# One pair of matmul products swapped in a seven-product loop, activation sums put in their order of use, and one value stage moved by a slot

## The chip, the core and the metric

The kernel runs on one core of a Trainium2 chip. The metric is the device time of that core in microseconds; the median of three executions before the change is 364.5 us (364.15 to 364.51). The profiled execution spans 361.7 us from its first to its last instruction, at a granted TensorE clock of 1.000.

## What is computed

Two layers follow each other. The first is a block-sorted attention on 4 batches of 8 heads, with sequences of 768 in 8 blocks of 96 and a head width of 64. The second is a mixture of 4 experts on the 3072 tokens that come out.

```python
# attention: P is 8x8 per head, from five rounds of row and column normalisation of exp(sort_net)
k_sorted = einsum('bhij,bhjcd->bhicd', P, k_blocks)      # blocks of keys mixed
v_sorted = einsum('bhij,bhjcd->bhicd', P, v_blocks)      # blocks of values mixed
attn = softmax(scale * q_block @ k_sorted_block.T)       # 96x96 inside each block
x = attn @ v_sorted_block                                # -> 3072 x 512

# experts: D = 512, F = 1024, E = 4
p = domain_probs / domain_probs.sum(-1)
out = sum(p[:, e] * (relu(x @ w1[e]) @ w2[e]) for e in range(4))
```

## The kernel before

The kernel's order is written out by hand: a manual schedule, in which each engine runs its instructions in the order in which the Python code emits them, and waits are put in where a tile is read, written or reused. Four batches, b = 0 to 3, have three chunks of 256 tokens each, c = 0 to 2; a chunk is also called group g = 3b + c. Attention of the next batches is computed in between the expert products of the present one. A chunk calls `slot()` after each of its pieces, and the tables `PLANS` (lines 614 to 641) say which attention stage runs in which slot: the entry `(0, 2, st_a, 2, 0)` in `PLANS[1]` runs stage `st_a` of batch 2, head pair 0, in slot 2 of chunk 0 of batch 1. The stages are `st_v` (line 357: two matmuls mix the values, ScalarE copies them to SBUF in line 367, and six small DMAs spread them into the tile `vs`), `st_k` (line 388, the keys), `st_s` (line 409: scores and exponential, two PSUM tiles), `st_a` (line 438: attention times values, one PSUM tile for each of two heads, evacuated by the `normalize` of line 427, which is a reciprocal and a multiplication on VectorE, lines 430 and 431) and `st_x` (line 457, a DMA transpose into the input of the experts). All of them take their PSUM tiles in turn from one pool with two buffers, `psA`.

The expert layers avoid part of their matmuls. Where a product of 2 x 2 blocks would take eight block products, the kernel takes seven (Strassen's method in Winograd's form) and pays with additions of blocks of weights and activations. Three pieces of code matter here.

**Chunks of batch 0 with c > 0** (`chunk`, lines 866 to 899). The second layer runs seven products by the function `times` (line 758), which accumulate over experts in four halves of PSUM banks, `bankA` to `bankQ`. The sums of activations are made by `h_sums` (line 744) on VectorE: number 1 is line 750, 2 is 752, 3 is 754, 4 is 756. The product "t2" adds into `bankA`, line 884 evacuates `bankA` into `oa2`, and the product "t3" then adds further into the same bank, so it has to wait for that evacuation. The sums number 3 and 4 stand ahead of line 884 in VectorE's queue. The product "t3" reads the sums number 3, the product "b22" behind it reads the sums number 4.

**The first layer of the last six groups** (`last_first` from line 1160, with `seven` from line 1080). Groups 6 to 11 are handled in three pairs, with one call of `last_first` for each pair and two of `last_second`. A pair has eight parts, two for each expert. Each part has seven products of four matmuls (line 1104), 128 x 128 weights by 256 columns, and three PSUM banks: X, Z (two of each, taken in turn by even and odd parts) and Q (four). The functions of a part are:

- `p1`: product into Z, then ScalarE copies Z into X (line 1124)
- `p5`: product into Q
- `p6`: product added into X, ScalarE copies X to `u2` (line 1131)
- `p2`: product added into Z, VectorE evacuates Z to the activations (`finish`, line 1110: relu and weight)
- `p7`: product added into X, ScalarE copies X to `u3` (line 1139), VectorE makes `t22` = Q + `u3` (line 1140)
- `p4`: product added into X, VectorE evacuates X (line 1110)
- `p3`: product added into Q, VectorE makes `t12` = Q + `u2` (line 1148)
- 22 and 12: `finish2` of `t22` and `t12`: relu on ScalarE (line 1116), weight on GpSimd (line 1117)

The loop of lines 1182 to 1194 interleaves a part (`now`) with the one before it (`prev`). In this document "now6" is `p6` of the present part and "prev4" is `p4` of the previous one. In the order of the code, a repeat has the products now1, prev7, now5, now2, now6, prev4, prev3, and ScalarE's order is line 1124 (now1), 1139 (prev7), 1116 (`t12`, two parts back), 1131 (now6), 1116 (`t22` of the previous part). The last part's `p7` follows the loop, and its `p4` and `p3` run inside `last_second`.

**The second layer of these groups** (`last_second`, line 1199). The products are emitted by its own `product` (line 1212, matmuls of line 1217). The fourth sums (line 1252), which overwrite the lower half of the activations, precede the third sums (line 1265). They are read by the product "b22", which comes in two portions: for the first experts ahead of the product "t3" (line 1268; `early` is 1 in the last group, else 2), for the other experts behind it (line 1282). The third sums are read by "t3".

Of the kernel before, what the change touches and what calls it, by code (L numbers as in the profile page):

```python
# [12 lines left out]
ALU = mybir.AluOpType  # L13
# [4 lines left out]
def kernel(  # L18
# [18 lines left out]
    E = moe_w1.shape[0]  # L37
# [571 lines left out]
    def st_bk(b, qd):  # L609
# [16 lines left out]
            (2, 9, st_k, 2, 0), (2, 9, st_lv, 3, 0), (2, 9, st_n, 3, 0), (2, 11, st_s, 2, 0), (2, 12, st_q, 2, 2),  # L626
        ],
        1: [
            (0, 0, st_k, 2, 1), (0, 0, st_bk, 2, 1), (0, 1, st_lk, 3, 0), (0, 1, st_n, 3, 1), (0, 2, st_a, 2, 0), (0, 2, st_q, 2, 3),
            (0, 3, st_v, 2, 2), (0, 3, st_n, 3, 2), (0, 4, st_s, 2, 1), (0, 4, st_x, 2, 0), (0, 5, st_k, 2, 2),  # L630
            (0, 5, st_n, 3, 3), (0, 6, st_v, 2, 3), (0, 6, st_lv, 3, 1), (0, 7, st_s, 2, 2), (0, 8, st_k, 2, 3),
            (0, 8, st_bv, 3, 0), (0, 9, st_bk, 3, 0), (0, 9, st_lk, 3, 1), (0, 9, st_q, 3, 0), (0, 10, st_a, 2, 1),
            (0, 11, st_s, 2, 3), (0, 12, st_a, 2, 2), (0, 12, st_x, 2, 1), (0, 12, st_q, 3, 1), (0, 13, st_v, 3, 0),
# [110 lines left out]
    def h_sums(e, which, own=False, hb=None):  # L744
        h = Hb[:, homes.get(e, e)] if hb is None else hb(e)
        blk = lambda kh, tok: h[:, ds(kh * KH, KH), ds(tok * P, P)]
        sm = [Sb[:, n, e].rearrange("p (f x) -> p f x", f=KH) for n in range(4)]
        tt = nc.vector.tensor_tensor
        if which == 1:
            tt(sm[0], blk(0, 1), blk(1, 1), ALU.add)  # L750
        elif which == 2:
            tt(sm[1], sm[0], blk(0, 0), ALU.subtract)
        elif which == 3:
            tt(blk(0, 1) if own else sm[2], blk(0, 0), blk(0, 1), ALU.subtract)
        else:
            tt(blk(1, 0) if own else sm[3], blk(1, 0), sm[1], ALU.subtract)

    def times(ps, lhs, rhs, es, first=True, done=True, between=None, at=None):

        for e in es:  # L760
            if e == at:
                between()
            for f in range(KH):
                nc.tensor.matmul(  # L764
                    ps, lhs(e, f), Ts[e][rhs][:, f, :],
                    start=(first and e == es[0] and f == 0), stop=(done and e == es[-1] and f == KH - 1),
                    skip_group_check=True,
                )
# [28 lines left out]
    def chunk(b, c, slot, done=()):  # L797
# [68 lines left out]
        if c:  # L866
            both = ob.rearrange("p (h d) -> p h d", h=2)
            times(bankA, blk(0, 0), "b11", es)
            slot()
            times(bankB, blk(1, 0), "b21", es)  # L870
            slot()
            tt(oa1, bankA, oa1, ALU.add)
            tt(oa1, bankB, oa1, ALU.add)
            h_sums(E - 1, 2)
            times(bankC, blk(1, 1), "n4", es[:1], True, False)
            times(bankQ, sm(0), "t1", es)
            tt(ob2, bankQ, ob2, ALU.add)
            slot()
            for e in es:
                h_sums(e, 3)  # L880
            for e in es:
                h_sums(e, 4)
            times(bankA, sm(1), "t2", es, False)
            tt(oa2, bankA, oa2, ALU.add)
            slot()
            next(sums0)
            times(bankC, blk(1, 1), "n4", es[1:], False)
            tt(ob1, bankC, ob1, ALU.add)
            slot()
            times(bankA, sm(2), "t3", es, False)  # L890
            tt(both, bankA.rearrange("p (o d) -> p o d", o=1).broadcast_to([P, 2, DH]), both, ALU.add)
            slot()
            store(1, ob)
            next(sums0)
            times(bankQ, sm(3), "b22", es, False)
            tt(oa2, bankQ, oa2, ALU.add)
            slot()
            store(0, oa)
            return
# [180 lines left out]
    def seven(g, n):  # L1080

        lead = g == G0
        if lead:
            e, f0, cols = n, 0, P
            pb = pbs[divmod(g, R // 2)]
            home = lambda i, j: Hb[:, e, ds(i * KH, KH), ds(j * P, P)]
            weight = lambda j: pb[:, ds(e, 1), ds(j * P, P)]
            n -= 1
            Q = last["Q"][(0, 0, 1, 3)[e]][:]
        else:  # L1090
            e, f0, cols = n // 2, n % 2 * 2, 2 * P
            home = lambda i, j: (last["H"][e] if j else Hb[:, e])[:, ds(i * KH + f0, 2), :]
            weight = lambda j: pbs[g](j, e)
            Q = last["Q"][n % 4][:]
        m = 512 // cols
        a, t = As[e], Bs[g]
        X, Z = [last[nm][n % len(last[nm])][:] for nm in ("X", "Z")]
        u2, u3, t22, t12 = [last[nm][n % len(last[nm])] for nm in ("u2", "u3", "t22", "t12")]
        tt = nc.vector.tensor_tensor

        def product(dst, lhs, rhs, first=False):
            for f in range(m):
                for k in range(2):
                    nc.tensor.matmul(  # L1104
                        dst[:, ds(f * cols, cols)], a[lhs][:, k, ds((f0 + f) * P, P)], t[rhs][:, k, :],
                        start=(first and f == 0 and k == 0), stop=(f == m - 1 and k == 1), skip_group_check=True,
                    )

        def finish(i, j, src):
            nc.vector.scalar_tensor_tensor(  # L1110
                out=home(i, j), in0=src.rearrange("p (f x) -> p f x", f=m), scalar=0.0,
                op0=ALU.max, in1=weight(j).broadcast_to([P, m, cols]), op1=ALU.mult,
            )

        def finish2(i, j, src):
            nc.scalar.activation(src, src, AF.Relu, bias=0.0, scale=1.0)  # L1116
            nc.gpsimd.tensor_tensor(  # L1117
                home(i, j), src.rearrange("p (f x) -> p f x", f=m),
                weight(j).broadcast_to([P, m, cols]), ALU.mult,
            )  # L1120

        def p1():
            product(Z, "a11", "b11", True)
            nc.scalar.copy(X, Z)  # L1124

        def p5():
            product(Q, "s1", "t1", True)

        def p6():
            product(X, "n2", "n2")  # L1130
            nc.scalar.copy(u2, X)  # L1131

        def p2():
            product(Z, "a12", "b21")
            finish(0, 0, Z)

        def p7():
            product(X, "s3", "t3")
            nc.scalar.copy(u3, X)  # L1139
            tt(t22, Q, u3, ALU.add)  # L1140

        def p4():
            product(X, "a22", "t4")
            finish(1, 0, X)

        def p3():
            product(Q, "s4", "b22")
            tt(t12, Q, u2, ALU.add)  # L1148

        return {  # L1150
            1: p1, 2: p2, 3: p3, 4: p4, 5: p5, 6: p6, 7: p7,
            22: lambda: finish2(1, 1, t22), 12: lambda: finish2(0, 1, t12),
        }

# [5 lines left out]
    def last_first(g, slot=None):  # L1160
        b, c = divmod(g, R // 2)
        lead = int(g == G0)
        if lead:
            chunk_first(b, c, [0], 0, slot)
            last_banks(0)
            last_tmp(g)
            prs = {1: seven(g, 1)}
            prs[1][1]()
            prs[1][5]()
            seven(g, 2)[5]()  # L1170
            prs[1][6]()
            prs[1][2]()
            input_sums(0, 0, True)
            input_sums(0, 1, True)
            last_banks(1)
        else:
            last["e0"][2]()
            prs = {0: last["e0"]}
        N7 = E if lead else 2 * E
        for e in range(1 + lead, N7):  # L1180
            prs[e] = seven(g, e)
        for e in range(1 + lead, N7):
            now, prev = prs[e], prs[e - 1]
            now[1]()
            prev[7]()
            if e > 1 + lead:
                prs[e - 2][12]()
            if not lead or e > 2:
                now[5]()
            now[2]()  # L1190
            now[6]()
            prev[22]()
            prev[4]()
            prev[3]()
        now[7]()
        prev[12]()
        return now

    def last_second(g, now=None, upper=False):
# [12 lines left out]
        def product(ps, lhs, rhs, first=True, es=range(E), between=None, at=E - 1, part=ds(0, DH)):  # L1212
            for e in es:
                if e == at and between:
                    between()
                for f in range(KH):
                    nc.tensor.matmul(  # L1217
                        ps, lhs(e, f), Ts[e][rhs][:, f, part],
                        start=(first and e == 0 and f == 0), stop=(e == E - 1 and f == KH - 1), skip_group_check=True,
                    )  # L1220
# [27 lines left out]
            sums(e, 2)  # L1248
        product(bankC, blk(1, 1), "n4")
        nc.scalar.copy(ob1, bankC)  # L1250
        for e in range(E):
            sums(e, 4, True)
        if lead:
            for e in range(E):
# [8 lines left out]
        if not lead:  # L1263
            for e in range(E):
                sums(e, 3, True)
        early = 1 if final else 2
        for bank, part, _ in ends:
            product(bank[:, part], blk(1, 0), "b22", False, range(early), part=part)
        if closing and not final:
# [201 lines left out]
```

The softmax here doesn't subtract the row's maximum and nothing guards it: scores larger than these inputs give would overflow.

## Time and profile before

| | |
|---|---|
| time, median of three | 364.5 us |
| span of the profiled execution | 361.7 us |
| `last_first` of the three pairs (first loop product to the first of `last_second`, by the timeline) | 211.1 to 233.4, and the same 49.4 and 98.8 us later |
| MATMUL of L1104 into X, Z, Q with 256 columns, each | 0.27 us drawn |
| ACT L1124, L1131, L1139, each | 0.57, 0.59, 0.59 us |
| ACT L1116, each | 0.63 us |
| DVE L1110, L1140, L1148, each | 0.68, 0.69, 0.68 us |
| ACT L367, each | 0.80 us |

PE is the matmul side of TensorE, PEld its loading of weights, DVE is VectorE, ACT ScalarE and POOL GpSimd. A line of the timeline gives the start of a run of equal instructions, its length to the drawn end of the last, engine, source line, operation, what it writes and reads, shapes, the number, and in brackets the idle time ahead of it with what ended that. The ends of matmuls are modelled and overlap; their starts are measured.

### The profile page before, as it was taken

The page shows a single profiled execution, that of the slowest core. Times are in us where ns is not written, and L with a number is a line of the kernel's source. Part 1 is how long each engine was busy: PE and PEld are TensorE (multiplying, and loading weights), DVE is VectorE, ACT ScalarE, POOL GpSimd, SP SyncE. Part 2 cuts the span into 40 slices and gives each one's busy share as a digit, 9 for nine tenths or more (in the row PEclk, how much of TensorE's full clock was granted, in tenths as well). Part 3 has the DMA queues.
Part 4 walks back from the last instruction along what each step waited for, and adds up shares of the span by engine and source line. Part 5 has one row for each costly group of instructions (what it writes and reads, how often), then busy time and mean ns, then how long its engine had stood idle before and what let it go on. Part 6 is the DMA issues. An engine that isn't in the chain of part 4 may idle for free.

```text
span 361.7 us, 9496 instructions
## 1 busy us (share of the span) xinstructions
PE 352.7 (98%) x3949; PEld 305.5 (84%) x3949; DVE 271.8 (75%) x549; ACT 172.6 (48%) x306; POOL 133.6 (37%) x148
## 2 busy tenths in 40 slices
PE   8799999999999999999999999999999999999995
PEld 8686857888888888988889888888888888888895
DVE  5653897769788777778878977895588876677962
ACT  2664430452324255368937158820388611688210
POOL 8872110466022330000626228840068700288300
PEclk9999999999999999999999999999999999999999
DMA  8999999999999999934994310004200015100011
GB/s 106 201 206 231 214 209 198 202 180 184 180 194 136 197 128 168 167 86 69 167 207 70 117 61 0 2 2 126 107 3 2 3 59 117 61 0 2 2 72 46
DMA packets 72007, 40.52 MB, mean 112 GB/s; under 512 B 40598, under 2 KB 66716, under 8 KB 71964
## 3 DMA queue, kind: packets, MB, share of 16 engines
q0 software_dynamic: 36560, 19.93, 41.0%
q1 hardware_dynamic: 35260, 19.92, 28.1%
q8 instruction: 31, 0.51, 0.6%
q14 instruction: 12, 0.10, 0.1%
q10 hardware_dynamic: 144, 0.07, 0.1%
HBM read 42.13 MB, written 6.34 MB: 134 GB/s over the span
## 4 chain that ended last, share of the span: by engine, by line
PE 87%; DMA 6%; DVE 3%; POOL 1%; SPq 1%; ACT 1%; issue 1%; ACTq 0%; DVEq 0%; POOLq 0%
PE ps_Q L1217 17%; PE ps_h L780 16%; PE ps_X L1104 10%; PE ps_p L764 8%; PE ps_Z L1104 7%; PE ps_Q L1104 7%; PE ps_Z L1217 6%; DMA w<-in_moe_w_dram 4%; PE ps_h L669 3%; PE ps_o L704 3%; PE ps_p L815 3%; DMA vs<-arena 2%; PE ps_a L449 1%; PE ps_s L414 1%; PE ps_v L361 1%; SPq L375 1%
## 5 line engine op out<-in xcount | busy, mean ns | idle before, releaser
L780 PE MATMUL ps_h<-xT,w 128*128 128x256 f16 x576 | 67.7, 273 | 0.0
L780 PEld LDWEIGHTS <-w 128*128 128x128 f16 x576 | 55.2, 98 | 7.3
L786 DVE SCALAR_TENSOR_TENSOR Hb<-ps_h,pb 128x1024 f16<-128x1024 f32 x34 | 41.5, 1223 | 17.1 <-PE ps_h L780 16.8
L1104 PEld LDWEIGHTS <-w 128*128 128x128 f16 x480 | 43.5, 98 | 6.4 <-issue 0.3
L1117 POOL TENSOR_TENSOR arena<-tmp,pb 128x512 f16<-128x512 f32 x12 | 15.3, 1276 | 65.8 <-PE ps_Z L1104 49.9
L1217 PEld LDWEIGHTS <-Hb 128*128 128x128 f16 x320 | 31.2, 98 | 3.6
L1116 ACT ACTIVATE tmp<-tmp 128x512 f32<-128x512 f32 x46 | 29.3, 637 | 3.2 <-DVE tmp L1148 2.6
L1217 PEld LDWEIGHTS <-Sb 128*128 128x128 f16 x304 | 28.2, 98 | 3.0
L421 ACT ACTIVATE ET<-ps_s 96x768 f16<-96x768 f32 x24 | 18.1, 802 | 25.4 <-PE ps_s L414 25.2
L1104 PEld LDWEIGHTS <-arena 128*128 128x128 f16 x312 | 27.7, 98 | 2.9
L404 ACT CAST kT<-ps_k 64x384 f16<-64x384 f32 x48 | 22.7, 473 | 14.1 <-PE ps_k L395 13.1
L121 POOL DMA_DIRECT2D arena<-in_q_dram x24 | 19.9, 840 | 19.0 <-DMA q_ring<-arena 18.4
L1104 PE MATMUL ps_X<-ET,arena 128*128 128x256 f16 x168 | 25.2, 272 | 0.0
L1124 ACT COPY ps_X<-ps_Z 128x512 f32<-128x512 f32 x27 | 15.4, 570 | 19.9 <-PE ps_Z L1104 15.6
L764 PEld LDWEIGHTS <-Hb 128*128 128x128 f16 x232 | 21.9, 98 | 3.0
L1217 PE MATMUL ps_Q<-w,Hb 128*128 128x256 f16 x192 | 24.4, 273 | 0.0
L1104 PE MATMUL ps_Z<-xT,w 128*128 128x256 f16 (+1 forms) x176 | 22.5, 258 | 0.2 <-ACT ps_X L1124 0.2
L1140 DVE TENSOR_TENSOR tmp<-ps_Q,tmp 128x512 f32<-128x512 f32 x20 | 13.8, 692 | 11.3 <-ACT tmp L1139 7.6
L1110 DVE SCALAR_TENSOR_TENSOR Hb<-ps_X,pb 128x512 f16<-128x512 f32 x27 | 18.4, 682 | 1.6 <-PE ps_X L1104 1.6
L1131 ACT COPY tmp<-ps_X 128x512 f32<-128x512 f32 x26 | 15.2, 586 | 9.0 <-PE ps_X L1104 8.7
L750 DVE TENSOR_TENSOR Sb<-Hb 128x512 f16<-128x512 f16 x33 | 19.5, 609 | 0.0
L1110 DVE SCALAR_TENSOR_TENSOR Hb<-ps_Z,pb 128x512 f16<-128x512 f32 x27 | 18.4, 682 | 1.3 <-PE ps_Z L1104 1.3
(261 smaller groups left out, 743.7 us busy)
## 6 DMA issues: line engine op xcount, KB each, us to landing
w<-in_moe_w_dram POOLq DMA_DIRECT2D x7, 1024.0 KB, 28.4
pb<-p_dram SPq DMA_DIRECT2D x9, 512.0 KB, 6.6
arena<-in_k_dram POOLq DMA_DIRECT2D x8, 384.0 KB, 10.0
arena<-in_v_dram POOLq DMA_DIRECT2D x8, 384.0 KB, 8.5
vs<-arena SPq DMA_DIRECT2D x36, 66.0 KB, 5.7
arena<-in_q_dram POOLq DMA_DIRECT2D x24, 96.0 KB, 8.1
out_dram<-ob SPq DMA_DIRECT2D x9, 256.0 KB, 2.1
out_dram<-oa SPq DMA_DIRECT2D x8, 256.0 KB, 2.3
```

What stands on the lines that cost most here:

```text
L121: nc.gpsimd.dma_start(t[:, h // 2, :, h % 2, :], q[b, h].rearrange("(t p) d -> p t d", p=P))
L404: nc.scalar.copy(kT[ds(D * hh, D), r], pk[ds(D * r, D), hh].rearrange("p a (i c) -> p a i c", c=CP),)
L421: nc.scalar.activation(ETs[2 * (pr % 2) + hh][:, 0:S].rearrange("c (a x) -> c a x", a=2), pss[hh][0:BLK, :, 0:HS], AF.Exp, bias=0.0, scale ...
L750: tt(sm[0], blk(0, 1), blk(1, 1), ALU.add)
L764: nc.tensor.matmul(ps, lhs(e, f), Ts[e][rhs][:, f, :], start=(first and e == es[0] and f == 0), stop=(done and e == es[-1] and f == KH - 1 ...
L780: nc.tensor.matmul(ps[:, f, :], w1sb[e][:, kc, ds((4 * g + f) * P, P)], xT[:, kc, ds(2 * c * P, 2 * P)], start=(kc == 0), stop=(kc == NKC ...
L786: nc.vector.scalar_tensor_tensor(out=Hb[:, homes.get(e, e), ds(4 * g, 4), :], in0=ps[:], scalar=0.0, op0=ALU.max, in1=weights(e).broadcast ...
L1104: nc.tensor.matmul(dst[:, ds(f * cols, cols)], a[lhs][:, k, ds((f0 + f) * P, P)], t[rhs][:, k, :], start=(first and f == 0 and k == 0), st ...
L1110: nc.vector.scalar_tensor_tensor(out=home(i, j), in0=src.rearrange("p (f x) -> p f x", f=m), scalar=0.0, op0=ALU.max, in1=weight(j).broadc ...
L1116: nc.scalar.activation(src, src, AF.Relu, bias=0.0, scale=1.0)
L1124: nc.scalar.copy(X, Z)
L1217: nc.tensor.matmul(ps, lhs(e, f), Ts[e][rhs][:, f, part], start=(first and e == 0 and f == 0), stop=(e == E - 1 and f == KH - 1), skip_gro ...
```

## The change

There are four edits. None adds or removes an instruction that computes; each changes places in the queues.

1. In `PLANS[1]`, `st_a` of batch 2, head pair 0, moves from slot 2 of chunk 0 to slot 3, behind the `st_v` of head pair 2 that was there. It gives the six DMAs of its values one slot more time.
2. In the chunks of batch 0 with c > 0, the product "t2" and its evacuation are emitted ahead of the fourth sums.
3. In the loop of `last_first`, for the pairs (not for group 5, the `lead` case), prev4 follows now2 directly and now6 comes behind it. The new function `p24` emits now2's product, then all of prev4 with its evacuation of X, and only then the evacuation of Z.
4. In `last_second`, again not for group 5, only the fourth sums of the first `early` experts precede the third sums; those of the other experts follow them.

```diff
-            (0, 0, st_k, 2, 1), (0, 0, st_bk, 2, 1), (0, 1, st_lk, 3, 0), (0, 1, st_n, 3, 1), (0, 2, st_a, 2, 0), (0, 2, st_q, 2, 3),
-            (0, 3, st_v, 2, 2), (0, 3, st_n, 3, 2), (0, 4, st_s, 2, 1), (0, 4, st_x, 2, 0), (0, 5, st_k, 2, 2),
+            (0, 0, st_k, 2, 1), (0, 0, st_bk, 2, 1), (0, 1, st_lk, 3, 0), (0, 1, st_n, 3, 1), (0, 2, st_q, 2, 3),
+            (0, 3, st_v, 2, 2), (0, 3, st_a, 2, 0), (0, 3, st_n, 3, 2), (0, 4, st_s, 2, 1), (0, 4, st_x, 2, 0), (0, 5, st_k, 2, 2),
...
             for e in es:
                 h_sums(e, 3)
+            times(bankA, sm(1), "t2", es, False)
+            tt(oa2, bankA, oa2, ALU.add)
             for e in es:
                 h_sums(e, 4)
-            times(bankA, sm(1), "t2", es, False)
-            tt(oa2, bankA, oa2, ALU.add)
             slot()
...
+        def p24(other):
+            product(Z, "a12", "b21")
+            other()
+            finish(0, 0, Z)
...
-            now[2]()
-            now[6]()
-            prev[22]()
-            prev[4]()
+            if lead:
+                now[2]()
+                now[6]()
+                prev[22]()
+                prev[4]()
+            else:
+                now[24](prev[4])
+                now[6]()
+                prev[22]()
             prev[3]()
...
-        for e in range(E):
+        early = 1 if final else 2
+        for e in range(E if lead else early):
             sums(e, 4, True)
...
         if not lead:
             for e in range(E):
                 sums(e, 3, True)
-        early = 1 if final else 2
+            for e in range(early, E):
+                sums(e, 4, True)
```

With that, ScalarE's order in a repeat stays as it was (lines 1124, 1139, 1116, 1131, 1116), and VectorE evacuates X ahead of Z.

More of the change, by code (lines that the diff above doesn't have):

```diff
@@ L1150, in seven @@
         return {
-            1: p1, 2: p2, 3: p3, 4: p4, 5: p5, 6: p6, 7: p7,
+            1: p1, 2: p2, 24: p24, 3: p3, 4: p4, 5: p5, 6: p6, 7: p7,
             22: lambda: finish2(1, 1, t22), 12: lambda: finish2(0, 1, t12),
```

## The prediction

> **What bounds the kernel now.** I read the page first, its busy line and then its chain.
>
> ```profile
> PE 352.7 (98%) x3949; PEld 305.5 (84%) x3949; DVE 271.8 (75%) x549; ACT 172.6 (48%) x306; POOL 133.6 (37%) x148
> ...
> PE 87%; DMA 6%; DVE 3%; POOL 1%; SPq 1%; ACT 1%; issue 1%; ACTq 0%; DVEq 0%; POOLq 0%
> ```
>
> TensorE sets the end: 98% busy, 87% of the chain, the same matmuls before and after. Only time in which it stands still between two matmuls counts. The idle column hides most of that, because a matmul is drawn 0.27 us long while full ones start 0.109 us apart. So I went to the timeline and compared starts: a product of four 256-column matmuls should take 0.44 us to the next.
>
> First, a repeat of the pair stage's loop (PE products there: L1104):
>
> ```profile
> 225.68 0.60 PE L1104 MATMUL ps_X<-ET,w 128*128 128x256 f16 x4
> 225.95 0.59 ACT L1131 COPY tmp<-ps_X 128x512 f32<-128x512 f32 x1 [0.16 <-PE ps_X L1104]
> 225.97 0.68 DVE L1110 SCALAR_TENSOR_TENSOR Hb<-ps_Z,pb 128x512 f16<-128x512 f32 x1
> ...
> 226.44 0.63 ACT L1116 ACTIVATE tmp<-tmp 128x512 f32<-128x512 f32 x1
> 226.55 0.60 PE L1104 MATMUL ps_Z<-xT,w 128*128 128x256 f16 x4
> 226.57 0.68 DVE L1110 SCALAR_TENSOR_TENSOR Hb<-ps_X,pb 128x512 f16<-128x512 f32 x1
> ...
> 227.36 0.57 ACT L1124 COPY ps_X<-ps_Z 128x512 f32<-128x512 f32 x1 [0.29 <-DVE Hb L1110]
> 227.42 0.60 PE L1104 MATMUL ps_Q<-kT,arena 128*128 128x256 f16 x4
> ...
> 227.84 0.59 ACT L1139 COPY room<-ps_X 128x512 f32<-128x512 f32 x1
> 227.98 0.60 PE L1104 MATMUL ps_Z<-xT,w 128*128 128x256 f16 x4
> ```
>
> The product at 227.98 (second of its part) should start at 227.86. It adds into Z, which L1124 copies until 227.93, and L1124 waited for DVE's eviction of X, begun at 226.57 behind that of Z. This loop of DVE and ACT takes 3.17 us (224.19 to 227.36) against 7 x 0.437 = 3.06 of products. By starts, a stage loses 0.04, 0.05, 0.12, 0.12, 0.12 in the loop and 0.04 at its last third-kind product: 0.49, in three stages 1.47 us.
>
> Second, the stage with the value change (b=1, first chunk):
>
> ```profile
> 121.23 2.35 PE L780 MATMUL ps_h<-xT,w 128*128 128x256 f16 x20
> ...
> 123.98 0.64 PE L449 MATMUL ps_a<-vs,ET 96*128 96x65 f16 x16 [0.40 <-DMA vs<-arena]
> ...
> 126.20 0.49 PE L361 MATMUL ps_v<-arena 128*128 128x384 f16 x2
> ...
> 126.77 0.80 ACT L367 CAST arena<-ps_v 128x768 f16<-128x768 f32 x1 [4.63 <-PE ps_v L361]
> ```
>
> Twenty matmuls from 121.23 end their turn at 123.41; L449 starts 0.56 later, for a DMA.
>
> Third, a chunk of b=0:
>
> ```profile
> 89.44 1.04 PE L764 MATMUL ps_p<-T,Hb 128*128 128x256 f16 x8
> ...
> 90.32 0.41 DVE L884 TENSOR_TENSOR room<-ps_p,room 128x256 f32<-128x256 f32 x1
> ...
> 90.79 1.47 PE L764 MATMUL ps_p<-T,Sb 128*128 128x256 f16 x12 [0.32 <-DVE room L884]
> ```
>
> Eight matmuls from 89.44 are through at 90.31; the next starts 0.48 later, for L884. In the next chunk the same place loses 0.18 (114.67 for 114.49).
>
> **The Trainium skill.** "PSUM — Partial Sum Buffer", Engine vs sequencer instructions: ScalarE and VectorE queues are strict FIFO, and matmuls start in program order. The trace agrees: every repeat runs L1124, L1139, L1116, L1131, L1116. The same page, PSUM bank collisions: guard PSUM by bank, so a product into X must await the whole copy out of X; here 0.05 us pass from L1124's end to the matmul (227.93 to 227.98). "ScalarE: Activation LUTs", What ACT_TABLE_LOAD costs: back-to-back ACTIVATEs overlap by about 93 ns; L1124 to L1139 shows 0.57 - 0.48 = 0.09. "Perfetto Trace Analysis", Per-engine timelines: a matmul's end is estimated, so I use starts.
>
> **The loop, part by part.** Products per repeat before: now1, prev7, now5, now2, now6, prev4, prev3. After: now1, prev7, now5, now2, prev4, now6, prev3. No instruction is added. DVE evicts X (prev4) ahead of Z (now2), which cuts the old DVE loop by 0.60: no longer the bound. But prev4 adds into the X bank that L1139 copies, and L1139 stands behind L1124. Before, three products lay between prev7 and prev4; now two. And now6 comes a product later, while its copy L1131, then a relu L1116, stand ahead of the next L1124 in ACT's queue; behind that L1124 wait now2 and everything after it on PE. This closes a new loop:
>
> - now6 to L1131: 0.71 (225.24 to 225.95)
> - L1131 to L1116: 0.48 (216.56 to 217.04; 0.49 above)
> - L1116 to L1124: back to back not in the trace. At most 0.63 + 0.08 (what L1131, with three waits, starts later behind its product than L1139 with one, 0.71 against 0.63); at least some 0.42 (0.63 less twice the overlap). I take 0.63 - 0.09 = 0.54
> - L1124 to L1139: 0.48
> - L1139: 0.59, and 0.05 to prev4
> - prev4 to now6: 0.44
>
> Sum 3.29 a repeat, 0.23 over PE's own 3.06. DVE keeps up: in a repeat it has 4 x 0.6 = 2.4.
>
> Whole stage, absolute, by the timeline from 211 us: at e=1 now2 starts at 212.37; L1139 (212.18 + 0.59 + 0.05) lets prev4 start at 212.82, now6 at 213.26. Six repeats later, the last now6 is at 213.26 + 6 x 3.29 = 233.00. The last prev7 then needs L1131's end, 0.71 + 0.59 + 0.05 = 1.35 after now6, with only prev3 between, where prev4 and prev3 were: 234.35. Before it was at 232.94. So +1.41 a stage, the old 0.49 already in it; three stages (from 211, 260 and 310) +4.23. With 0.42: +0.69 a stage; with 0.71: +2.43.
>
> **The value stage.** The group before now ends at E = 125.16 and the value product takes 0.33. The DMA is long there, so 0.56 is saved. But the pool psA has two buffers. The attention's first head takes one; its second needs the one that the value product filled, free when L367 ends: E + 0.57 + 0.80, and 0.05. Without that it starts at E + 0.57: 0.85 lost. Then 0.24 of attention, 1.75 of products: E + 3.41, where the scores' two heads need both buffers again, and TensorE with all that follows waits for them. DVE has L786 from E + 0.20 (1.13 to the next), two sums (0.44, 0.34), then two normalisations of 0.84 that ran earlier before: done at E + 3.88. The scores' second matmul, due at E + 3.5, loses 0.4. Net 0.85 + 0.40 - 0.56 = +0.69 (0.3 to 1.0).
>
> **The order of sums.** In the b=0 chunks the eviction (now ahead of three L756 sums) comes when the "t2" product ends, 89.26 in the trace, so it is over by 89.8, ahead of 90.31: -0.48, and -0.18 in the other chunk. The eviction now waits on DVE for the product's end; behind it stand the three L756 sums, L735 and L888. The sums are due only after twelve more matmuls (1.3 us against their 1.1), L888's bank only in the next group. -0.66 (-0.3 to -0.7).
>
> In the second half of the pair stages the fourth sums of late experts go behind the third sums. PE shows no wait for a sum there; its one gap, 0.23 at 354.68, is for ACT's L1262. All are still done within the 8 and 16 matmuls ahead of their use: 0.
>
> Sum: 4.23 + 0.69 - 0.66 = 4.26; 364.5 + 4.3 = 368.8.
>
> **Rivals.**
> 1. Faster: ACT overlaps so much that its loop falls under 3.06; PE never waits there. For it: the visible bound, X's eviction, is cut by 0.60. Against: ACT's sum would have to lose 0.23. -1.47 + 0.03: 363.1. Chance 0.11.
> 2. A milder loop, with the relu only 0.42 ahead of L1124: 3 x 0.69 + 0.03 = 2.1: 366.6. For it: none of the trace's ACT pairs is like this one. Chance 0.10.
> 3. A harder loop, each three-wait copy dispatched only after the relu's end: 3 x 2.43 + 0.03 = 7.3: 371.8. For it: L1131's extra 0.08. Chance 0.09.
>
> **How the numbers follow.** The main case has 0.70: 368.8, whose spread from the value stage and the sums is about 0.5 and from the loop's terms (0.03 in each of 18 repeats) 0.5. The range takes in rival 2 and ends between the main case and rival 3: 366.2 to 370.9, leaving out rival 1 and 3. Faster by over 0.2% (under 363.8): rival 1 and a little of a lucky sum, 0.12. Within: 0.04. Slower: 0.84.
>
> **What would show it.** Right: in the loop, L1124 follows an L1116 directly and no longer waits for DVE, prev4 starts 0.05 behind L1139's end, repeats last 3.3; the waits name ACT ahead of PE; L449 splits in two with a gap of 0.8 for L367; L764 follows L764 at once in the chunks of b=0. Wrong: repeats of 3.06 (ACT takes less than its rows say), or another order of ACT's instructions.

## The result and the profile after

The kernel after the change takes 368.4 us (median of six executions, 368.04 to 368.48), the kernel before 364.2 us (median of six, 362.69 to 364.51). The ratio is 1.0119 with a 95% interval of 1.0102 to 1.0137: slower by 4.2 us; 368.8 was predicted. The profiled execution spans 366.5 us against 361.7. Medians are of all executions of a kernel, while executions more than 1.5% above its fastest are left out of the ratios and of the spreads given below.

Line numbers move a little with the diff. In the kernel after, `p7`'s copy of X (1139 before) is L1144, the sums for `t22` and `t12` (1140, 1148) are L1145 and L1153, and the matmuls of `last_second` (1217) are L1227. L1104, L1110, L1116, L1124 and L1131 keep their numbers.

The page of the kernel after, its busy line and its chain:

```profile
PE 357.7 (98%) x3949; PEld 306.8 (84%) x3949; DVE 272.0 (74%) x549; ACT 170.8 (47%) x306; POOL 133.0 (36%) x148
...
PE 91%; DMA 3%; DVE 2%; ACT 1%; POOL 1%; issue 1%; ACTq 0%; DVEq 0%; POOLq 0%
```

These two lines name no new bound. The same 3949 matmuls are drawn 5.0 us longer, because most of a late start is hidden under the drawn end of the matmul ahead. The chain puts no more on ScalarE (ACT) than before. As before, the starts have to be read.

One repeat of the pair stage's loop after the change, from the timeline (start, length to the drawn end, engine, line, what is written and read):

```profile
226.63 0.60 PE L1104 MATMUL ps_X<-ET,arena 128*128 128x256 f16 x4
...
226.85 0.68 DVE L1110 SCALAR_TENSOR_TENSOR Hb<-ps_X,pb 128x512 f16<-128x512 f32 x1
...
227.34 0.58 ACT L1131 COPY tmp<-ps_X 128x512 f32<-128x512 f32 x1 [0.67 <-PE ps_X L1104]
...
227.83 0.63 ACT L1116 ACTIVATE tmp<-tmp 128x512 f32<-128x512 f32 x1
...
228.36 0.59 ACT L1124 COPY ps_X<-ps_Z 128x512 f32<-128x512 f32 x1
...
228.87 0.59 ACT L1144 COPY room<-ps_X 128x512 f32<-128x512 f32 x1
229.00 0.60 PE L1104 MATMUL ps_Z<-xT,w 128*128 128x256 f16 x4
...
229.51 0.60 PE L1104 MATMUL ps_X<-ET,w 128*128 128x256 f16 x4
...
229.95 0.27 PE L1104 MATMUL ps_X<-ET,arena 128*128 128x256 f16 x1
```

The loop can be followed from now6 to now6. The product now6 starts at 226.63, its copy L1131 at 227.34, the relu L1116 at 227.83, L1124 directly behind it at 228.36, the copy L1144 at 228.87. That copy ends at 229.46, prev4 starts at 229.51, and the next now6 at 229.95. The repeat lasts 3.32 us where seven products take 3.06. The product now2 at 229.00 waits as well (L1124 ends at 228.95), so the lost time is split over two places, 0.15 ahead of now2 and 0.08 ahead of prev4, with 0.04 ahead of a prev7.

VectorE is out of this loop. X is evacuated at 226.85, as soon as its product allows, and that ends 0.83 us before L1124 starts. The view of line L1124 says the same; it lists durations (shortest, median, longest, in ns) and until what its engine sat idle ahead of it (us, times). First the row of the kernel before that changes, then the kernel after:

```profile
  DVE Hb L1110: 4.3, 16
```

```profile
L1124 ACT COPY ps_X<-ps_Z x27: 570/589/592, 187.8 to 333.5; 128x512 f32<-128x512 f32 x27
...
  PE ps_Z L1104: 15.1, 8
  DVE Hb L1110: 0.3, 1
```

Before, VectorE's eviction released L1124 16 times. After, it does so once. But L1124 is now idle ahead only 9 times of 27: the other 18 times (six repeats in each of three stages) it starts right behind another ScalarE instruction. ScalarE's own queue has become what L1124 waits for.

The last prev7 of the first pair stage, in the timeline after:

```profile
234.62 0.60 PE L1104 MATMUL ps_X<-ET,arena 128*128 128x256 f16 x4 [0.31 <-ACT tmp L1131]
```

The last now6 is at 233.27, and this prev7 must await its copy, until 234.62, with only prev3 in between: 0.48 lost. From its first product into Z to the first of `last_second`, the stage runs from 211.19 to 235.05, 23.86 us; before it ran from 211.06 to 233.37, 22.31. That is +1.55 for each of three stages, +4.65. The second and third stage show the same shift.

The value stage after:

```profile
124.55 0.49 PE L361 MATMUL ps_v<-arena 128*128 128x384 f16 x2
...
125.12 0.80 ACT L367 CAST arena<-ps_v 128x768 f16<-128x768 f32 x1 [3.59 <-PE ps_v L361]
...
125.97 0.40 PE L449 MATMUL ps_a<-vs,ET 96*128 96x65 f16 x8 [0.69 <-ACT arena L367]
...
128.50 0.51 PE L414 MATMUL ps_s<-q_ring,kT 64*128 64x96 f16 x15 [0.23 <-DVE xsl L431]
```

The wait for the DMA is gone: the first head follows the value product at 124.88. The second head of L449, at 125.97, waits for L367 to release its buffer (by starts 0.85 late), and the second matmul of the scores for the second normalisation, which runs from 127.75 to 128.44 (it starts 0.44 behind the first, some 0.4 late).

A chunk of batch 0 after:

```profile
89.36 0.42 DVE L882 TENSOR_TENSOR room<-ps_p,room 128x256 f32<-128x256 f32 x1
...
89.48 1.04 PE L764 MATMUL ps_p<-T,Hb 128*128 128x256 f16 x8
...
90.36 1.36 PE L764 MATMUL ps_p<-T,Sb 128*128 128x256 f16 x11
```

The eviction (L882 here) runs while the eight matmuls do, ahead of the L756 sums (89.70), and "t3" follows the matmuls at once. The 0.48 and the 0.18 of the two chunks are gone. In the last pair's second half the 0.23 for ScalarE's evacuation is still there, now at 359.45; no other wait appeared in these stages.

### The profile page after: what moved, and what is told of

Read it like the earlier page. It is cut to its first block, busy times and chain, and to the rows that moved or that the text cites. A ratio compares the mean times of both kernels' runs of the same rounds, so it can differ in the third digit from the quotient of the medians.

```text
span 366.5 us, 9495 instructions
## 1 busy us (share of the span) xinstructions
PE 357.7 (98%) x3949; PEld 306.8 (84%) x3949; DVE 272.0 (74%) x549; ACT 170.8 (47%) x306; POOL 133.0 (36%) x148
## 4 chain that ended last, share of the span: by engine, by line
PE 91%; DMA 3%; DVE 2%; ACT 1%; POOL 1%; issue 1%; ACTq 0%; DVEq 0%; POOLq 0%
PE ps_Q L1227 17%; PE ps_h L780 17%; PE ps_p L764 11%; PE ps_X L1104 10%; PE ps_Z L1104 7%; PE ps_Z L1227 6%; PE ps_Q L1104 6%; PE ps_h L669 3%; DMA arena<-in_v_dram 3%; PE ps_o L704 3%; PE ps_p L815 3%; PE ps_s L414 2%; PE ps_a L449 1%; PE ps_k L395 1%; PE ps_v L361 1%
## 5 line engine op out<-in xcount | busy, mean ns | idle before, releaser
L786 DVE SCALAR_TENSOR_TENSOR Hb<-ps_h,pb 128x1024 f16<-128x1024 f32 x34 | 41.5, 1223 | 17.6 <-PE ps_h L780 17.6
L1104 PEld LDWEIGHTS <-w 128*128 128x128 f16 x480 | 43.3, 97 | 9.3 <-issue 3.2
L1227 PEld LDWEIGHTS <-Hb 128*128 128x128 f16 x320 | 31.2, 98 | 3.5
L1104 PEld LDWEIGHTS <-arena 128*128 128x128 f16 x312 | 27.6, 97 | 4.8 <-issue 1.5
L1116 ACT ACTIVATE tmp<-tmp 128x512 f32<-128x512 f32 x46 | 29.2, 634 | 3.5 <-DVE tmp L1153 2.6
L1227 PEld LDWEIGHTS <-Sb 128*128 128x128 f16 x304 | 28.2, 98 | 3.0
L1104 PE MATMUL ps_X<-ET,arena 128*128 128x256 f16 x168 | 25.1, 272 | 0.9 <-ACT tmp L1131 0.9
L1145 DVE TENSOR_TENSOR tmp<-ps_Q,tmp 128x512 f32<-128x512 f32 x20 | 13.8, 691 | 14.6 <-ACT tmp L1144 14.6
L1227 PE MATMUL ps_Q<-w,Hb 128*128 128x256 f16 x192 | 24.4, 273 | 0.0
L1131 ACT COPY tmp<-ps_X 128x512 f32<-128x512 f32 x26 | 15.2, 585 | 19.5 <-PE ps_X L1104 19.5
L1124 ACT COPY ps_X<-ps_Z 128x512 f32<-128x512 f32 x27 | 15.7, 583 | 15.4 <-PE ps_Z L1104 15.1
L1104 PE MATMUL ps_Z<-xT,w 128*128 128x256 f16 (+1 forms) x176 | 22.5, 257 | 0.2 <-ACT ps_X L1124 0.2
L1110 DVE SCALAR_TENSOR_TENSOR Hb<-ps_X,pb 128x512 f16<-128x512 f32 x27 | 18.5, 686 | 1.6 <-PE ps_X L1104 1.6
L1110 DVE SCALAR_TENSOR_TENSOR Hb<-ps_Z,pb 128x512 f16<-128x512 f32 x27 | 18.4, 682 | 1.3 <-PE ps_Z L1104 1.3
L750 DVE TENSOR_TENSOR Sb<-Hb 128x512 f16<-128x512 f16 x33 | 19.0, 594 | 0.0
```

What stands on the lines that cost most here:

```text
L786: nc.vector.scalar_tensor_tensor(out=Hb[:, homes.get(e, e), ds(4 * g, 4), :], in0=ps[:], scalar=0.0, op0=ALU.max, in1=weights(e).broadcast ...
L1104: nc.tensor.matmul(dst[:, ds(f * cols, cols)], a[lhs][:, k, ds((f0 + f) * P, P)], t[rhs][:, k, :], start=(first and f == 0 and k == 0), st ...
L1110: nc.vector.scalar_tensor_tensor(out=home(i, j), in0=src.rearrange("p (f x) -> p f x", f=m), scalar=0.0, op0=ALU.max, in1=weight(j).broadc ...
L1227: nc.tensor.matmul(ps, lhs(e, f), Ts[e][rhs][:, f, part], start=(first and e == 0 and f == 0), stop=(e == E - 1 and f == KH - 1), skip_gro ...
```

## The experiments

Each ran beside the kernel before on the same chip, and its ratio is to that kernel. The runs fall into three groups, each on a chip of its own, on which the kernel before takes 364.2 us (parts 1 to 3), 364.2 (parts 4 and 5 and the second run of part 2) and 364.4 (part 6). Diffs are against the kernel before unless something else is said. "By starts" means the time from one matmul's start to the next, less what the same form takes when nothing holds it.

### 1. Only the loop, and everything but the loop

Edit 3 alone, as in the change:

```diff
+            if lead:
+                now[2]()
+                now[6]()
+                prev[22]()
+                prev[4]()
+            else:
+                now[24](prev[4])
+                now[6]()
+                prev[22]()
```

> The kernel before with the loop's edit alone (now2, prev4, now6, X evicted ahead of Z). Theory 1 (ScalarE's queue closes a loop of 3.31 us through now6, L1131, L1116, L1124, L1139's line, prev4): a stage grows by about 1.55 us as in the changed kernel, three by 4.6, so 364.2 + 4.6 = 368.8. Rival (the growth comes mostly from the value stage and from the sums of the second half): clearly less, under 366.5.

Measured: 368.8 us, ratio 1.0132 (1.0101 to 1.0163).

Edits 1, 2 and 4 without edit 3, against the kernel after:

```diff
-            else:
-                now[24](prev[4])
-                now[6]()
-                prev[22]()
+            now[2]()
+            now[6]()
+            prev[22]()
+            prev[4]()
```

> The changed kernel without the loop's edit: value stage, order of sums in batch 0, fourth sums in the second half. Theory 1: +0.73 (0.85 + 0.44 lost, 0.56 saved) - 0.66 + 0 = +0.1, so 364.3. Rival: 366 or more.

Measured: 363.7 us, ratio 0.9994 (0.9975 to 1.0012). Its loop shows the stalls of the kernel before again (0.04, 0.05, 0.12, 0.12, 0.12, and 0.04 at the last product).

So edit 3 is the whole loss, within the intervals, and the other three together change nothing that can be measured.

### 2. The order of the products or that of the evictions?

Edit 3 does two things at once: it moves prev4 ahead of now6 on TensorE, and the eviction of X ahead of that of Z on VectorE. Two runs part them. In the first, against the kernel after, all four edits stay, but VectorE evicts Z ahead of X as before:

```diff
         def p24(other):
             product(Z, "a12", "b21")
-            other()
             finish(0, 0, Z)
+            other()
```

> The changed kernel with VectorE's evictions in the loop in their old order (Z ahead of X), the products staying in the new order. Theory 1 (ScalarE bounds the new loop, VectorE doesn't): X is then free some 2.1 us behind the end of the copy to u3, the next L1124 starts 2.2 us behind it, so the time stays within 0.3 us of the changed kernel, 368.4. Rival (VectorE's order of evictions sets the loop's pace): 0.6 us more in each repeat, some 18 repeats, over 375.

Measured: 368.6 us, ratio 1.0146 (1.0099 to 1.0194), as after. (A stretch of its profiled execution ahead of the loop, at 120 to 123 us, has a DMA wait and matmuls twice as far apart; its span is not compared.) Its loop by the timeline:

```profile
223.37 0.60 PE L1104 MATMUL ps_Z<-xT,w 128*128 128x256 f16 x4
...
224.47 0.68 DVE L1110 SCALAR_TENSOR_TENSOR Hb<-ps_Z,pb 128x512 f16<-128x512 f32 x1
...
225.07 0.68 DVE L1110 SCALAR_TENSOR_TENSOR Hb<-ps_X,pb 128x512 f16<-128x512 f32 x1
...
225.51 0.64 ACT L1116 ACTIVATE room<-room 128x512 f32<-128x512 f32 x1
...
226.04 0.59 ACT L1124 COPY ps_X<-ps_Z 128x512 f32<-128x512 f32 x1
...
226.68 0.60 PE L1104 MATMUL ps_Z<-xT,w 128*128 128x256 f16 x4
```

The eviction of Z starts at 224.47 and that of X behind it; it is over at 225.75, and L1124 still starts at 226.04 only, 0.53 behind the relu at 225.51. The repeat, 223.37 to 226.68, is 3.31. With the new order of products VectorE's order is worth nothing.

In the second, edit 3 alone is made and the products keep their old order; only the evictions change places:

```diff
+        def p24(other):
+            product(Z, "a12", "b21")
+            other()
+            finish(0, 0, Z)
...
+            else:
+                now[24](lambda: (now[6](), prev[22](), prev[4]()))
```

> The kernel before with the products of the loop in their old order (now2, now6, prev4, prev3) and VectorE's evictions alone swapped, X (prev4) ahead of Z (now2). Theory 1: the old loop of 3.17 us through X's eviction is cut by 0.60, ScalarE's chain from now6 to now2 stays 2.8, so TensorE runs at 3.06 a repeat; of the 0.49 a stage, 0.45 goes, three stages 1.35 faster: 362.8. Rival (the eviction of Z, now later, becomes the bound, or the swap of evictions is what hurt in the changed kernel): the same time or slower.

Measured: 362.2 us, ratio 0.9953 (0.9937 to 0.9970). This is faster than the kernel before, by 1.7 us. A repeat of it:

```profile
223.54 0.59 ACT L1131 COPY tmp<-ps_X 128x512 f32<-128x512 f32 x1
...
224.03 0.64 ACT L1116 ACTIVATE tmp<-tmp 128x512 f32<-128x512 f32 x1
...
224.82 0.57 ACT L1124 COPY ps_X<-ps_Z 128x512 f32<-128x512 f32 x1 [0.16 <-PE ps_Z L1104]
...
225.45 0.60 PE L1104 MATMUL ps_Z<-xT,w 128*128 128x256 f16 x4
...
228.51 0.60 PE L1104 MATMUL ps_Z<-xT,w 128*128 128x256 f16 x4
```

The copy L1131 starts at 223.54, earlier in the repeat than after, as now6 does. The relu is done at 224.67, and L1124 waits for its own product and for nothing else. The repeat, 225.45 to 228.51, is 3.06: TensorE's own time. From the first L1124 of a pair to the first of the next, 48.88 us pass (209.99 to 258.87) against 49.33 before (209.13 to 258.46): 0.45 less for this stage, and by the starts 1.3 in three.

So the loss is the order of the products alone, and the gain that was there to be had lay in the order of the evictions alone.

### 3. Is it the relu ahead of L1124?

If the loop runs through ScalarE's queue, taking the relu out from between L1131 and L1124 must open it. Against the kernel after, the relu and weight of `t22` go one repeat later, behind the next L1124 and L1144:

```diff
             if e > 1 + lead:
+                if not lead:
+                    prs[e - 2][22]()
                 prs[e - 2][12]()
...
                 now[24](prev[4])
                 now[6]()
-                prev[22]()
...
         now[7]()
+        if not lead:
+            prev[22]()
```

> The changed kernel with the relu of t22 (L1116, finish2 of the previous part) emitted one repeat later, behind the next L1124 and the copy to u3, so that it no longer stands between L1131 and L1124 on ScalarE. Theory 1: the loop of ScalarE loses 0.53, 3.31 to 2.8, under TensorE's 3.06; what stays is about 0.05 a repeat (prev4 still waits for the copy to u3 by now1 0.68 + 0.52 + 0.59 + 0.05 against four products) and 0.48 at the stage's end: some 0.85 a stage against 2.05 now, so 3.6 less, 364.8. Rival (now6 coming a product later and prev4's wait are what costs, wherever the relu stands): within 1 us of the changed kernel's 368.4.

Measured: 365.6 us, ratio 1.0048 (1.0028 to 1.0067): 2.8 us back of the 4.2, where 3.6 were expected. The intervals of the two ratios would allow the missing 0.8 to be noise, but the traces show where it went. In the loop the effect is what was expected:

```profile
218.06 0.60 PE L1104 MATMUL ps_Z<-xT,w 128*128 128x256 f16 x4
...
220.52 0.57 ACT L1124 COPY ps_X<-ps_Z 128x512 f32<-128x512 f32 x1 [0.26 <-DVE Hb L1110]
...
221.19 0.60 PE L1104 MATMUL ps_Z<-xT,w 128*128 128x256 f16 x4
```

The product now2 at 218.06 is followed by the next at 221.19, 3.13 later, and L1124 is no longer right behind a relu. It starts 0.68 behind its product (219.84 to 220.52); the view names VectorE, but where only the evictions changed the same 0.68 passes (224.14 to 224.82). By starts a stage loses 0.04 here and there, 0.25 in the loop, and 0.48 at the last prev7, which still has only prev3 ahead of it. What was missed is a new wait in the second half. The trace of this kernel there:

```profile
234.60 5.32 POOL L1117 TENSOR_TENSOR tmp<-tmp,pb 128x512 f16<-128x512 f32 x4 [0.55 <-ACT tmp L1116]
236.71 3.49 DVE L750 TENSOR_TENSOR Sb<-Hb 128x512 f16<-128x512 f16 x3
...
240.46 0.41 DVE L750 TENSOR_TENSOR Sb<-Hb 128x512 f16<-128x512 f16 x1
```

And the same place in the kernel after:

```profile
238.55 2.42 DVE L750 TENSOR_TENSOR Sb<-Hb 128x512 f16<-128x512 f16 x3
```

With one relu more behind the loop, GpSimd has four multiplications without a pause where after it had three, and a pause ahead of the fourth. In both traces a sum of L750 on VectorE is drawn 0.41 us long when no multiplication of GpSimd runs beside it, and 1.48 when one does for 1.2 us or more. Here two of the sums are of that length (at 237.31 and 238.72), in the kernel after one (at 239.48). The first three sums thus spread over 3.49 us instead of 2.42, and the fourth comes at 240.46. A matmul on these sums starts at 240.93, 0.06 behind that sum's end, and 0.22 late; one ahead of it is 0.06 late. In the other two stages the two are 0.12 and 0.22. These 1.0 us in all account for the 0.8 that were missed. The loop through the relu is shown; taking it out this way moves part of the cost.

### 4. The value stage

Edit 1 alone:

```diff
-            (0, 2, st_a, 2, 0), (0, 2, st_q, 2, 3),
-            (0, 3, st_v, 2, 2), (0, 3, st_n, 3, 2),
+            (0, 2, st_q, 2, 3),
+            (0, 3, st_v, 2, 2), (0, 3, st_a, 2, 0), (0, 3, st_n, 3, 2),
```

> The kernel before with the first edit alone (st_a of batch 2 a slot later, behind st_v). Theory: 0.56 of the DMA's wait saved, 0.85 for the PSUM buffer and 0.44 at the scores lost: 0.73 slower. Rival (the saved wait is the larger): 0.2 to 0.5 faster.

Measured: 364.3 us, ratio 1.0012 (0.9998 to 1.0027), +0.44 with an interval of -0.1 to +1.0. The trace has the two waits of the kernel after, to the hundredth: the second head (127.12) is 0.85 late, and the scores' second matmul (129.64) starts 0.44 behind the first.

Which of the two comes from the buffer and which from VectorE? Moving `st_v` into slot 2 and `st_a` alone into slot 3 parts the two heads from the value product, so that the buffer is free; the normalisations still come a slot late:

```diff
-            (0, 2, st_a, 2, 0), (0, 2, st_q, 2, 3),
-            (0, 3, st_v, 2, 2), (0, 3, st_n, 3, 2),
+            (0, 2, st_v, 2, 2), (0, 2, st_q, 2, 3),
+            (0, 3, st_a, 2, 0), (0, 3, st_n, 3, 2),
```

> The kernel before with st_v and st_a of the value stage exchanged: st_v in slot 2, st_a in slot 3, so that the second head of st_a finds its PSUM buffer free. Theory 2 (behind the buffer's wait stands VectorE's queue, L786, two sums and two normalisations, 4.0 us from the group's end to the scores' second matmul): removing the buffer's wait gains nothing, the scores wait some 1.6 us instead; 0.33 later still for the value product that now precedes the group: 1.06 slower than before. Rival (the PSUM buffer's 0.85 is a cost of its own): 0.1 faster than before.

Measured: 364.7 us, ratio 1.0029 (1.0014 to 1.0044), +1.06.

```profile
125.10 0.65 PE L449 MATMUL ps_a<-vs,ET 96*128 96x65 f16 x16
...
128.21 0.21 PE L414 MATMUL ps_s<-q_ring,kT 64*128 64x96 f16 x1 [0.71 <-DVE xsl L431]
129.05 0.51 PE L414 MATMUL ps_s<-q_ring,kT 64*128 64x96 f16 x15 [0.62 <-DVE xsl L431]
```

Both heads run in one piece at 125.10 and neither waits for a DMA or a buffer: that is what the slot was meant to give. But the scores now lose 0.87 and 0.81, both for L431. VectorE's queue (L786, two sums, two normalisations) sets when the scores can start, and in the kernel after the stall of L449 only takes part of that wait in advance. A slot later is a slot too late for VectorE, with or without the shared buffer.

### 5. The order of the sums

Edit 2 alone:

```diff
-            for e in es:
-                h_sums(e, 4)
             times(bankA, sm(1), "t2", es, False)
             tt(oa2, bankA, oa2, ALU.add)
+            for e in es:
+                h_sums(e, 4)
```

> The kernel before with the second edit alone (t2's product and the eviction of bankA ahead of the fourth sums in batch 0). Theory: the two waits for that eviction, 0.48 and 0.18 us, go, and no other comes: 0.66 faster. Rival (the fourth sums, now later, hold up the product b22, or VectorE's backlog moves to the next chunk): no gain.

Measured: 363.8 us, ratio 0.9999 (0.9980 to 1.0017), with executions from 362.1 to 367.0. The time doesn't resolve 0.66 us. The trace does: L882 starts at 89.32 and "t3" at 90.31, 0.87 behind the product ahead of it, and neither of the two old waits is left. The kernel before spreads nearly as far on this chip, 362.4 to 366.7, so the spread needs no cause in the edit. What can cause it is seen in the waits of TensorE in this profile (engine, line, what it waited for: sum, times, longest):

```profile
PE ps_h L780 <- DMA xT<-xsl: 1.9, 1, 1.9
```

This wait for a transposing DMA, 2.03 us by starts at 120.74, isn't in the profile of before. A second one, 1.20 at 99.00, is for L786, which began 2.3 us later than in the kernel after (97.72 for 95.41) with its product through:

```profile
87.44 0.70 SPq L213 DMA_DIRECT2D pb<-p_dram  x1
...
97.72 2.35 DVE L786 SCALAR_TENSOR_TENSOR Hb<-ps_h,pb 128x1024 f16<-128x1024 f32 x2 [2.61 <-PE ps_h L780]
```

L786 also reads `pb`, the experts' probabilities for the tokens of a chunk. Their load by line 213 landed at 97.63, 10.2 us behind its issue and 0.09 ahead of L786; in the kernel after it was issued at 85.92 and landed at 93.94, 8.0 us behind. So this wait was for a DMA as well, though the view names the matmul.

### 6. What is best of it

The evictions swapped with the products in the old order (the second run of part 2), and edit 2:

```diff
+            else:
+                now[24](lambda: (now[6](), prev[22](), prev[4]()))
...
+            times(bankA, sm(1), "t2", es, False)
+            tt(oa2, bankA, oa2, ALU.add)
             for e in es:
                 h_sums(e, 4)
```

> The kernel before with two edits: VectorE's evictions in the loop swapped (X ahead of Z, products in their old order) and t2's eviction ahead of the fourth sums in batch 0. Theory: the gains add, 1.3 and 0.66: some 2.0 faster than before, ratio 0.9945. Rival (a gain in batch 0 is given back at the value stage's DMA, which lands no earlier): 1.3 to 1.5 faster, ratio 0.996.

Measured: 362.6 us, ratio 0.9950 (0.9933 to 0.9967): 1.8 us faster (1.2 to 2.4), which doesn't part the theory from the rival.

All four edits, except that the products keep their old order, against the kernel after:

```diff
             else:
-                now[24](prev[4])
-                now[6]()
-                prev[22]()
+                now[24](lambda: (now[6](), prev[22](), prev[4]()))
```

> The changed kernel with the products of the loop in their old order and only the evictions swapped: all four edits but for the place of prev4. Theory 1 (the place of prev4 alone makes the changed kernel slow): 368.4 - 4.6 - 1.3 = 362.5 on the chip of those runs, ratio to before 0.997. Rival (the edits disturb each other): 1.000 or more.

Measured: 362.3 us, ratio 0.9944 (0.9924 to 0.9963), where 0.997 was expected. Edit 1 was booked there at its cost of 0.7 us. Its two waits are in the trace (0.85 and 0.41), but the time shows no loss; the next section says what this can mean. The two kernels of this part and that of the evictions alone can't be told apart by their times. All three beat the kernel before by 1.7 to 2.0 us and the kernel after by about 6.

## Why the prediction was right, point by point

**TensorE bounds, by starts.** Right. Busy time and chain name no culprit, before or after; by starts the loop's 4.65, the value stage's 0.7 and the sums' -0.66 make 4.7 of the 4.8 us by which the profiled span grew.

**The new loop through ScalarE.** Right, and it is the whole loss (experiments 1 to 3). Term by term, with the repeat shown above:

| step | predicted | measured |
|---|---|---|
| now6 to L1131 | 0.71 | 0.71 |
| L1131 to L1116 | 0.48 | 0.49 |
| L1116 to L1124 | 0.54 (0.42 to 0.71) | 0.53 |
| L1124 to the copy behind it | 0.48 | 0.51 |
| copy, and 0.05 to prev4 | 0.64 | 0.64 |
| prev4 to now6 | 0.44 | 0.44 |
| sum | 3.29 | 3.32 |

The term that no row showed, a relu followed by L1124, came out as the relu's 0.63 less 0.10. That is close to the overlap for back-to-back ACTIVATEs in the Trainium skill ("ScalarE: Activation LUTs", What ACT_TABLE_LOAD costs: about 93 ns; here 102 to 105 ns, but only 74 to 77 between L1124 and the copy behind it), and it settles the rivals: neither the 0.42 of the milder loop nor the 0.71 of the harder one, and the faster one, under 3.06 a repeat, fell with them.

**The size of a stage.** +1.41 predicted, +1.55 measured. The first now6 (213.39) came 2.20 us after the stage's first product, as worked out, and the last prev7 1.35 after the last now6, as worked out. Between them lie 19.88 us where six times 3.29 make 19.74. The whole 0.14 is thus the repeat: 3.31 in the mean, and the mis-sized term is L1124 to the copy, taken at 0.48 from a trace in which L1124 always started after a pause. Three stages: 4.65 for 4.23.

**VectorE keeps up.** Right: with the evictions the other way round the repeats last as long.

**The value stage.** Both added waits were right: 0.85 and some 0.4 for 0.85 and 0.40, and the second normalisation ends 3.89 after the group's end, for 3.88. The saved wait, 0.56, was read from one execution, and it isn't one number. In the kernels without edit 1 the wait at L449 differs:

```profile
126.03 0.64 PE L449 MATMUL ps_a<-vs,ET 96*128 96x65 f16 x16 [1.64 <-DMA vs<-arena]
```

This is the kernel with the loop alone, 1.81 us; with the evictions alone it is 1.51; 1.47 with the evictions and sums; none in the one with the sums alone, which had lost 2.03 to another DMA shortly before. In each of the four with a wait, the kernel before among them, L449 starts 0.09 behind the landing of the last of its six DMAs, and that DMA took 6.6 us from issue to landing in the kernel before and 8.1, 7.8 and 7.6 in the other three. So the edit trades a wait of 0 to 1.8 us, which differs between executions, for a fixed 1.26. What it is worth in the mean isn't settled: its own run gives +0.4 (-0.1 to +1.0), and the run with all but the swap suggests less. An estimate of the saved wait in the mean is 1.26 - 0.44 = 0.8 from its own run and 1.68 - 1.06 = 0.6 from the exchange of stages, each uncertain by about 0.6. The prediction's 0.3 to 1.0 left out that the cost might be nothing.

**The sums.** -0.66 predicted; both waits are gone in every trace with the edit, to the hundredth. In time it isn't resolved. **Edit 4** changed no wait, as said.

**The sum.** 4.65 for the loop less 0.66 for the sums leaves 0.2 of the 4.2 for edit 1, where 0.69 was booked, if the sums gave in time what they gave in the traces. That the sum came within 0.1 of the measured 4.2 is thus in part luck: two misses of opposite sign, 0.42 too little for the loop, and 0.2 to 0.5 too much for the rest, the value stage as it seems, which is known only to about 0.6.

## What to carry to other kernels

Before a product is moved later, follow what is queued behind its evacuation: here one place in TensorE's order held back a copy, that copy a relu, the relu the next part's first copy, and the loop so closed was longer than the one it was meant to cut. Where an order of products and an order of evictions come together, try them apart: the gain was in VectorE's order and the loss in TensorE's. And a DMA wait read from a single profile is a sample, not a cost.

## What was not expected of the hardware

The same DMA wait at the same place varied between 0.56 and 1.81 us in four profiles of kernels that are alike up to there, apart from the sums of batch 0; in two further profiles TensorE waited 2.0 and 2.6 us for a transposing DMA that elsewhere showed no wait at all. The stretch ahead of all four edits varies too: the first matmul of line 704 starts at 27.8 to 29.6 us in the twelve profiles. Waits of this size fit the spread of the executions of the kernel before; that they make up all of it wasn't shown.

L1124 was drawn 570 ns long in all 27 cases before and 589 in the median after, where 18 of 27 follow another ScalarE instruction without a pause. The step from it to the copy behind it grew from 0.48 to 0.51 with that. In the kernel with only the evictions changed, where L1124 waits for its product again, it is 570 throughout.
